# A linear-attention layer gated by a GLU on one core: the down stage's operands loaded ahead from shared half buffers, two sets of down weights' sums moved between passes, folds of q re-spaced

## The chip, the cores and the metric

The kernel runs on one core of a Trainium2 chip. The metric is device time in microseconds (us) of one launch. The core has five engines with a queue each, which take their instructions in order: TensorE (PE, matmuls), VectorE (DVE), ScalarE (ACT), GpSimd (POOL), and SyncE (SP), which issues nearly all the DMAs of this kernel.

## The reference

With x of 2048 rows and 1024 columns, F = 3584, 32 heads of 32:

```python
xn = layernorm(x)
q, k, v = heads(xn @ wqkv)
phi_q = concat(softmax(q @ w_phi), softmax(-(q @ w_phi)))      # phi_k likewise
kv, z = sum_s phi_k[s] v[s], sum_s phi_k[s]
s = concat_heads((phi_q @ kv) / (phi_q @ z + 1e-6)) @ wo
h = sigmoid(xn @ w_gate) * (xn @ w_up)
out = x + s * silu(h @ w_down)
```

All is float32. The kernel makes each float32 product of three matmuls: an operand is split into a rounded part (a cast on ScalarE, L134) and the remainder (a subtraction on VectorE, L135), and L143, L144 and L145 multiply the three pairs that matter.

## The kernel before

**Stages.** Around the big products stands a two by two block scheme with seven products instead of eight (the names B11, B21, B22, T1 to T4), whose operands are sums and differences of blocks. The projections of q, k and v come first, then pass 1 of the gate and up products, then pass 2 (about 1350 to 1640 us), then the down product (to about 2120 us), then the output product and the gate.

**Pass 2** has *nests*: for an f block (128 of the 3584 columns) the T1 operand is itself made by seven products of quarter blocks, `nest(n, f)`. Its weights are loaded by `nest_load` (L518 and L520, from wg_d) and summed on GpSimd four ticks later (L524 to L527); `prep` then splits them with L134 and L135, for the next nest while TensorE is on this one. Inside a nest ScalarE copies banks from one product's place to the next (L1520, L1526, L1538, L1553), and TensorE starts the next product behind such a copy.

**Around it**, GpSimd multiplies the gates (L1415, L1530) and makes the sums of h for the down product (`h_out`, L1385 to L1388); SyncE stores them to h_d (L1378, L1382 and, three ticks later, L1392) and fetches the partial results m_d (L1362).

**Sums of down weights.** The seven down weights of each j in 0..13 are blocks of w_down (B11, B21, B22), or sums of four. `wd_sums(j, b)` loads four blocks (L885), subtracts four times on GpSimd (L875 to L878) four ticks later, and stores four results to wd_d (L882) seven ticks later. j of `WD_B` are made in pass 1 among the groups of sums of w_gu (`glu_group`, `wd_group`), those of `WD_C` in pass 2 every 11 ticks from the 20th, the last four in the down stage.

**Order.** A list `plan` maps ticks to functions; `later(n, f)` puts f n ticks ahead, and `tick()` is called between products. What a tick issues is put behind the last matmul and the latest instructions of VectorE, ScalarE and SyncE at that moment.

**Down stage.** `dsteps` holds 98 steps: 84 with both column halves of h (c = 0, 1) and 14 with one. `down_prep` prepares the next step whenever buffers for splits are free: it loads a weight (L898, 256 KB, from w_down or wd_d) into one of two halves of slot 42, and h (L904, 512 KB for both c; L908, 256 KB, for one) into one of slots 39, 40 and 41, and emits the splits in the same call. The loads of q for the attention (`q_late`) run in this stage on the same queue. SBUF is a row of `slots`, each with two halves; `raw_free` holds the free halves that pass 2's loads share.

**Folds of q**: `fold_steps(at, k)` makes, for a quarter k of the q weights, the products with the feature map, the transforms and the sums.

Of the kernel before, what the change touches and what calls it, by code (L numbers as in the profile page):

```python
# [49 lines left out]
def hedgehog_glu_kernel(  # L50
# [60 lines left out]
    NW = 8  # L111
    WARM = 57
    EARLY = 12
    BEHIND = 'DVE', 'Activation', 'SP'

    banks = [psum.tile([P, HB], F32, name=f"bank{i}") for i in range(8)]

    def whole(i):
        return slots[i].rearrange("p a n -> p (a n)")

    def halves(*ids):
        return [slots[i][:, a] for i in ids for a in range(2)]
# [6 lines left out]
    def pair(i):  # L129
        return slots[i][:, 0], slots[i][:, 1]  # L130
# [39 lines left out]
    def tick():  # L170

        clock[0] += 1
        with behind():
            glu_group()
            nest_load()
            for f, a in sorted(plan.pop(clock[0], []), key=lambda fa: fa[0] is fetch_operand):
                f(*a)

# [198 lines left out]
    def fold_keep(which, k, i, b):  # L377
        nc.sync.dma_start(wf_d[which, i, :, k], b)

    def fold_steps(at, k):  # L380

        def load():
            for n in range(4):
                fold_load(Q, k, n)

        def transforms():
            for n, o in enumerate(halves(*fblock[Q][k])):
                ps = tps.next()
                folded(Q, k, n, ps)
                nc.scalar.copy(o, ps)  # L390

        def sums():
            a11, a12, a21, a22 = bs = halves(*fblock[Q][k])
            for i, b in ((B11, a11), (B21, a12), (T4, a22)):
                fold_keep(Q, k, i, b)
            w_sums(lambda i, b: None, *bs)

        def keep():
            a11, a12, a21, a22 = halves(*fblock[Q][k])
            for i, b in ((T2, a11), (T3, a21), (T1, a22), (B22, a12)):  # L400
                fold_keep(Q, k, i, b)

        for n, f in ((0, load), (4, transforms), (6, sums), (8, keep)):
            later(at + n, f)


# [19 lines left out]
    summed = (T2, T3, T1, B22)  # L426

    FLY = range(2, NJ - 1)
    WD_B, WD_C = range(4), range(4, 10)
    raw_free, spare, groups, made_sums = deque(), [], deque(), {}  # L430
    for f in FLY:
        groups.extend((f, s) for s in range(2))
        if 0 <= f - 4 < len(WD_B):
# [3 lines left out]
    def glu_load(n):  # L437

        if n == len(ops) or ops[n][0] != "glu" or n in wraw:
            return True  # L440
        _, p, f, i = ops[n]
        if p == 1 and f in FLY:
            return True
        src = wg_d[summed.index(i), f] if i in summed else w_gu[f + NJ * (i == T4), int(i != B11)]
        if p == 0:
            r = gr.next()
            last_load[:] = [nc.sync.dma_start(whole(r), src).ins]
            wraw[n] = halves(r)
            return True
        if (p, f, i) == (1, 0, T2):  # L450
            raw_free.extend(halves(41, 42, 39, 40))
        if len(raw_free) < 2:
            return False
        wraw[n] = [raw_free.popleft() for _ in range(2)]
        for s, o in enumerate(wraw[n]):
            last_load[:] = [nc.sync.dma_start(o, src[:, s * HB:(s + 1) * HB]).ins]
        if (p, f, i) == (1, 1, T4):
            spare.extend(halves(43, 44))
            raw_free.extend(spare)
        return True  # L460

# [394 lines left out]
    dsteps = [(i, j, (0, 1)) for i in order[:-1] for j in range(NJ)]  # L856
    dsteps += [(B22, j, (c,)) for c in (0, 1) for j in range(NJ)]
    dready, hfree, wfree = [], deque(), deque()
    hraw = Ring((39, 40, 41))
    wdraw = Ring(halves(42))  # L860
    yr = Ring(halves(47, 48, 49))
    sig_r = Ring([slots[53][:, 0]])
    last_split, down_load = [], []

    def wd_block(i, j):
        f, col = {B11: (2 * j, 0), B21: (2 * j + 1, 0), B22: (2 * j + 1, 1)}.get(i, (2 * j, 1))
# [21 lines left out]
    def wd_sums(j, b):  # L888
        for n, f in zip((4, 7), wd_parts(j, b)):
            later(n, f)  # L890

    def down_prep():
        n = len(dready)
        if n == len(dsteps) or not wfree or len(hfree) < len(dsteps[n][2]):
            return False
        i, j, cs = dsteps[n]
        r = wdraw.next()
        down_load[:] = [nc.sync.dma_start(r, wd_block(i, j) if i in (B11, B21, B22) else wd_d[i, j]).ins]  # L898
        w = wfree.popleft()
        split(pair(w), r)  # L900
        r = hraw.next()
        hs = {}
        if len(cs) == 2:
            nc.sync.dma_start(whole(r), h_d[i, j].rearrange("p c n -> p (c n)"))  # L904
        for c in cs:
            rc = slots[r][:, c]
            if len(cs) == 1:
                nc.sync.dma_start(rc, h_d[i, j, :, c])  # L908
            hs[c] = hfree.popleft()
            last_split[:] = [split(pair(hs[c]), rc).ins]  # L910
        dready.append((w, hs))
        return True


# [507 lines left out]
    def begin_projection(c):  # L1422

        if c == 0:
            for k in range(4):
                fold_steps((1, 2, 5, 6)[k], k)
            for k in range(4):
                o_steps(14 + 10 * k, k, halves(52, 53))
            return
        for t in range(EARLY):  # L1430
            k_steps(1 + 72 * t // EARLY, 0, t)
        for n in range(5):
            queue2(17 + 8 * n, glu_sums, *sums.popleft(), halves(43, 44))

    def begin_pass(p):

        if p == 0:
            for n in range(CTT):
                later(1 + n + 4 * (n > 3), x_stats, n)
            later(19, x_scales)  # L1440
            for q in range(4):
                later(20 + q, x_rows, q)
            for u in range(4):
                later(24 + 12 * u, x_pair, u)
            for n in range(2 * CTT):
                q_steps(2 + 13 * n // 2, n // 2, n % 2)
            queue2(6, glu_sums, *sums.popleft(), halves(43, 44))
        elif p == 1:
            gates_r.items = halves(45, 46)
            gates_r.n = 0  # L1450
            for n, f, *a in ((165, x_nest_load, 0), (166, x_nest_load, 1), (166, x_nest_load, 2), (171, x_nest_load, 3), (170, x_nest_sums, 0),
                             (175, x_nest_sums, 1), (176, x_nest_split, T2), (177, x_nest_split, T3), (179, x_nest_split, T4)):
                later(n, f, *a)
            at = 1
            for t in range(EARLY, 2 * TT):
                k_steps(int(at), *divmod(t, TT))
                at += 7
                if t % TT == TT - 1:
                    k_end(int(at) + 8, t // TT)
                    at += 16  # L1460
        else:
            for n, j in enumerate(WD_C):
                queue2(20 + 11 * n, wd_sums, j, halves(53, 54))

    NEST = {B11: 4, B21: 6, B22: 2, T1: 0, T2: 16, T3: 18, T4: 36}

# [107 lines left out]
    for n, (kind, c, what, i) in enumerate(ops):  # L1574
# [88 lines left out]
                tick()  # L1663
        if flow["item"] == len(items) and flow["made"] - flow["used"] < NW:
            hfree.extend(ws)
            while wfree and down_prep():
                pass

        if phase == 0:
# [32 lines left out]
    for b in range(2):  # L1702
        block(f"x{b}", 4 * b, 4, F32)
    block("x6", 24, 4, F32)
    block("fb", 44, 3, F32)
    qraw.items = [slots[53][:, 1], slots[44][:, 0]]
    yr.items = halves(47, 48, 49, 27)
    eqr.items, zb = [50, 51, 24, 25], (whole(54), whole(26))
    u1, u2 = halves(0, 1, 2, 3), halves(4, 5, 6, 7)
# [12 lines left out]
    def evacuate(i, p):  # L1722

        b = banks[p]
        t = p // 4 * CTT + p % 4
        if i == B11:
            nc.scalar.copy(u1[p], b)
        elif i == B21:
            y = yr.next()
            nc.vector.tensor_copy(y, b)  # L1730
            nc.scalar.copy(b, u1[p])
            later(1 + (p + 1) // 2, gate_out, y, t, 0)
        elif i in (T2, T3):
            nc.scalar.copy((u1 if i == T2 else u2)[p], b)
        elif i == T4:
            gate_out(yr.next(), t + 4, 0, b)
        elif i == T1:
            nc.vector.tensor_add(u2[p], u2[p], b)
            later(1 + 2 * p, gate_out, u2[p], t + 4, 1)
        else:  # L1740
            nc.vector.tensor_add(u1[p], u1[p], b)
            gate_out(u1[p], t, 1)

    ND = len(dsteps)
    for n, j in enumerate(range(10, NJ)):
        later(1 + 14 * n, wd_sums, j, halves(43, 38))
    for hb in range(2):
        later(1 + hb, nc.sync.dma_start, zb[hb], zb_d[hb])
    for n in range(TT):
# [2 lines left out]
    for n, (i, j, cs) in enumerate(dsteps):  # L1752
        w, hs = dready[n]
        if (i, j) == (T2, 0):
            sig_r.items = [slots[53][:, 0]] + halves(38)
        for c in cs:
            for u in range(4):
                p = 4 * c + u
# [7 lines left out]
        hfree.extend(hs.values())  # L1766
        k, odd = divmod(n - (ND - 2 * NJ) - 9, 3)
        if not odd and 0 <= k < 4:

            with tc.issue_after(down_load[0]):  # L1770
                wo_prep(T3, k)
        if n >= ND - 2 * NJ - 8 and len(WO[B21]) < 4 and hfree:
            WO[B21].append(hfree.popleft())
# [7 lines left out]
            wo_prep(*divmod((n - 40) // 2, 4))  # L1781
        if n == ND - 2 * NJ:
            assert len(WO[B21]) == 4
            block("x1", 4, 4, F32R)
            side.extend([lambda k=k: wo_prep(B21, k) for k in range(4)])
            side.extend([lambda u=u: e_load(u) for u in range(2)])
        if n == ND - NJ:
            assert not plan
            block("x6", 24, 4, F32R)
            block("fb", 44, 3, F32R)  # L1790
            step(1000)
            side.extend([lambda fn=fn, a=a: fn(*a) for fn, *a in attend()])
        if len(dready) == ND:
# [2 lines left out]
                    WO[i].append(free.popleft())  # L1796
                    side.append(lambda i=i, k=len(WO[i]) - 1: wo_prep(i, k))
        if n > ND - 2 * NJ:
            step(1 + (n > ND - NJ and n % 2))
    step(1000)  # L1800
    assert len(WO[T1]) == len(WO[T4]) == 4
    block("fa", 39, 4, F32R)
# [169 lines left out]
```

## Time and profile before

| | |
|---|---|
| runs | 2371.30, 2371.32, 2372.62 us, median 2371.32 |
| profiled execution | 2373.14 us, its span 2371.40 us, granted clock 0.996 |
| busy | PE 2348.0 us (99%), PEld 1958.6, DVE 1649.0 (70%), ACT 1182.1 (50%), POOL 1046.7 (44%) |
| DMA | 633.55 MB, mean 267 GB/s, 76.2% of 16 engines |
| chain that ended last | PE 93%, DMA 2%, POOL 1%, DVE 1%, issue 1%, ACT 1% |

The span is the part of the launch that the profile covers; what lies around it is the difference to the time. "L143 <- ACT L1538" reads: the instruction of line 143 waited for the instruction of line 1538 on ScalarE.

### The profile page before, as it was taken

Reading aid. Unit: us, or ns where it says so; the run is one execution under the profiler, and the core shown is the slowest. Engines: PE = TensorE matmul, PEld = TensorE weight load, DVE = VectorE, ACT = ScalarE, POOL = GpSimd, SP = SyncE. Lnnn points to the kernel's source line nnn. Section 1 sums busy time; section 2 is a strip of 40 time slices with the busy share of each in tenths; the row PEclk is TensorE's granted clock in tenths of the full one; section 3 lists DMA queues with packets and bytes.
Section 4 is the critical chain, followed back from the end, with each engine's and each line's share of the span. In section 5 each row is a group of like instructions: output and inputs, shape, how many; then the busy total and the mean of one; then the engine's idle time right before and its main releaser. Section 6 shows DMA issues by size and latency. Waiting matters only on the chain.

```text
span 2371.4 us, 32110 instructions
## 1 busy us (share of the span) xinstructions
PE 2348.0 (99%) x10900; PEld 1958.6 (83%) x10900; DVE 1649.0 (70%) x2083; ACT 1182.1 (50%) x1848; POOL 1046.7 (44%) x737
## 2 busy tenths in 40 slices
PE   9999999999999999999999999989999999999999
PEld 8888888888888888888888888768888888888887
DVE  7625557755688855567766866545989888867776
ACT  7344544454645655555555555433445444355553
POOL 0314216731121044656421777774656343424556
PEclk9999999999999999999999999999999999999999
DMA  8789989976787776887674978779867667776665
GB/s 295 257 305 358 340 302 349 379 277 212 250 281 258 252 275 234 310 290 266 231 234 156 332 266 266 263 259 385 275 243 264 222 214 242 257 254 242 207 202 181
DMA packets 288309, 633.55 MB, mean 267 GB/s; under 512 B 36752, under 2 KB 37008, under 8 KB 283536
## 3 DMA queue, kind: packets, MB, share of 16 engines
q1 hardware_dynamic: 288144, 631.50, 76.2%
q8 instruction: 85, 1.39, 0.2%
q14 instruction: 80, 0.66, 0.1%
HBM read 378.40 MB, written 252.97 MB: 266 GB/s over the span
## 4 chain that ended last, share of the span: by engine, by line
PE 93%; DMA 2%; POOL 1%; DVE 1%; issue 1%; ACT 1%; SPq 0%; POOLq 0%; DVEq 0%; ACTq 0%
PE bank L143 29%; PE bank L144 29%; PE bank L145 29%; PE bank L727 1%; PE bank L375 1%; PE bank L1050 1%; PE bank L1026 1%; PE bank L1300 1%; DMA fc<-w_down 1%; DMA fc<-e_d 1%; DMA h_d<-x 0%; DMA fb<-wqkT 0%; PE bank L243 0%; POOL x L1415 0%; DMA fc<-qkv_d 0%
## 5 line engine op out<-in xcount | busy, mean ns | idle before, releaser
L143 PE MATMUL bank<-x,w 128*128 128x512 f32 x2304 | 898.9, 390 | 7.1 <-ACT bank L1538 7.0
L144 PE MATMUL bank<-x,w 128*128 128x512 f32 x2304 | 898.9, 390 | 0.0
L145 PE MATMUL bank<-x,w 128*128 128x512 f32 x2304 | 897.0, 390 | 0.0
L135 DVE TENSOR_TENSOR w<-fa,w 128x512 fp32r<-128x512 f32 (+2 forms) x437 | 426.8, 984 | 371.5 <-ACT w L134 363.0
L134 ACT CAST w<-fa 128x512 fp32r<-128x512 f32 (+2 forms) x437 | 296.6, 682 | 445.2 <-PE bank L144 345.6
L143 PEld LDWEIGHTS bank<-x,w 128*128 128x128 f32 x2304 | 433.7, 188 | 97.8 <-ACT bank L1538 7.8
L145 PEld LDWEIGHTS bank<-x,w 128*128 128x128 f32 x2304 | 433.6, 188 | 89.9
L144 PEld LDWEIGHTS bank<-x,w 128*128 128x128 f32 x2304 | 433.8, 188 | 89.2 <-DVE x L135 0.4
L143 PE MATMUL bank<-w,x 128*128 128x512 f32 x708 | 277.4, 392 | 0.0
L145 PE MATMUL bank<-w,x 128*128 128x512 f32 x708 | 276.0, 390 | 0.0
L144 PE MATMUL bank<-w,x 128*128 128x512 f32 x708 | 275.9, 390 | 0.0
L145 PEld LDWEIGHTS bank<-w,x 128*128 128x128 f32 x708 | 133.0, 188 | 27.5 <-DVE x L1226 0.3
L144 PEld LDWEIGHTS bank<-w,x 128*128 128x128 f32 x708 | 133.1, 188 | 26.4
L143 PEld LDWEIGHTS bank<-w,x 128*128 128x128 f32 x708 | 133.1, 188 | 26.2
L1370 ACT COPY fc<-bank 128x512 f32<-128x512 f32 x168 | 97.1, 582 | 96.8 <-PE bank L145 52.9
L135 DVE TENSOR_TENSOR x<-fa,x 128x512 fp32r<-128x512 f32 x112 | 105.0, 938 | 28.1 <-ACT x L134 27.8
L134 ACT CAST x<-fa 128x512 fp32r<-128x512 f32 x112 | 69.1, 617 | 61.6 <-DMA fa<-w_down 36.8
L135 DVE TENSOR_TENSOR w<-fb,w 128x512 fp32r<-128x512 f32 (+1 forms) x45 | 40.3, 894 | 48.6 <-ACT w L134 48.6
L1064 POOL TENSOR_TENSOR fc<-fc 128x512 f32<-128x512 f32 x32 | 48.9, 1528 | 56.3 <-DVE fc L1059 20.7
L135 DVE TENSOR_TENSOR p<-fc,p 128x512 fp32r<-128x512 f32 (+1 forms) x67 | 52.2, 790 | 30.6 <-ACT p L134 29.7
L135 DVE TENSOR_TENSOR x<-fb,x 128x1024 fp32r<-128x1024 f32 x36 | 46.1, 1282 | 28.8 <-ACT x L134 28.7
L306 POOL TENSOR_TENSOR fb<-fb 128x512 f32<-128x512 f32 x6 | 8.4, 1396 | 126.3 <-DMA fb<-w_gu 116.9
(393 smaller groups left out, 3576.6 us busy)
## 6 DMA issues: line engine op xcount, KB each, us to landing
m_d<-fc SPq DMA_DIRECT2D x168, 256.0 KB, 3.6
fa<-h_d SPq DMA_DIRECT2D x84, 512.0 KB, 4.3
fa<-wf_d SPq DMA_DIRECT2D x32, 1024.0 KB, 6.3
x<-m_d SPq DMA_DIRECT2D x124, 256.0 KB, 5.0
h_d<-fc SPq DMA_DIRECT2D x104, 256.0 KB, 3.8
fc<-e_d SPq DMA_DIRECT2D x48, 512.0 KB, 5.1
fc<-qkv_d SPq DMA_DIRECT2D x72, 256.0 KB, 4.9
fa<-w_down SPq DMA_DIRECT2D x67, 256.0 KB, 4.1
```

What stands on the lines that cost most here:

```text
L134: nc.scalar.copy(o[0], src)
L135: i = nc.vector.tensor_sub(o[1], src, o[0].bitcast(F32))
L143: nc.tensor.matmul(o, a[0], b[0], start=first, stop=False, **kw)
L144: nc.tensor.matmul(o, a[0], b[1], start=False, stop=False, **kw)
L145: last_mm[:] = [nc.tensor.matmul(o, a[1], b[0], start=False, stop=last, **kw).ins]
L375: nc.tensor.matmul(ps[:, gs], r[:, gs], bd[:, 4 * f + g], start=True, stop=True)
L727: nc.tensor.matmul(kvb[g // 2][:, g % 2 * 256:g % 2 * 256 + 256], v[:, g].rearrange("p a f -> p (a f)"), ph[:, g].rearrange("p a f -> p (a ...
L1026: nc.tensor.transpose(ps[:, j * P:(j + 1) * P], e[:, k * P:(k + 1) * P], ident)
L1050: nc.tensor.matmul(ps[:, j * 256:(j + 1) * 256], kg[:, k], ph[:, a, k], start=a == 0, stop=a == 1)
L1064: nc.gpsimd.tensor_sub(o, a, b)
L1300: nc.tensor.transpose(banks[3][:, a % 4 * P:(a % 4 + 1) * P], ident, ident)
L1370: nc.scalar.copy(o, banks[b])
```

## The change

It does four things.

1. The loads of a down step are parted from its splits. `down_load` takes two or three halves from `raw_free` and issues the load of the weight and one 256 KB load for each half of h; `tick` calls it once the nests' loads are all out. `down_prep` splits a step at least `LEAD` = 2 ticks after its load and gives the halves back. Two halves (slot 44) are kept back at the end for the attention. The rings `hraw` and `wdraw` go.
2. `WD_B` grows from 4 to 6 sets, made in pass 1; the other four of pass 2 come every 16 ticks instead of every 11.
3. The folds of q: the transforms of k = 2, 3 come one tick later, the output folds at 16 + 9k instead of 14 + 10k.
4. Buffers that the attention and the last wd_sums use change place (slots 45 and 46 for 43 and 44), sigmoids get two buffers earlier, the last gates go out one tick instead of two ticks apart.

```diff
+    LEAD = 2
...
             nest_load()
+            if not nests:
+                glu_load(len(ops) - 1)
+            while down_load():
+                pass
...
-    def fold_steps(at, k):
+    def fold_steps(at, k, lead=4):
...
-        for n, f in ((0, load), (4, transforms), (6, sums), (8, keep)):
+        for n, f in ((0, load), (lead, transforms), (lead + 2, sums), (lead + 4, keep)):
...
-    WD_B, WD_C = range(4), range(4, 10)
+    WD_B, WD_C = range(6), range(6, 10)
...
-    hraw = Ring((39, 40, 41))
-    wdraw = Ring(halves(42))
+    ND = len(dsteps)
...
+    def down_back(o):
+        if len(down_loads) > ND - NJ and len(retired) < 2 and any(o is b for b in last_raw):
+            retired.append(o)
+        else:
+            raw_free.append(o)
+
+    def down_load():
+        n = len(down_loads)
+        if nests or len(ops) - 1 not in wraw or n == len(dsteps) or len(raw_free) < 1 + len(dsteps[n][2]):
+            return False
+        i, j, cs = dsteps[n]
+        r, *hr = [raw_free.popleft() for _ in range(1 + len(cs))]
+        last_down[:] = [nc.sync.dma_start(r, wd_block(i, j) if i in (B11, B21, B22) else wd_d[i, j]).ins]
+        for c, o in zip(cs, hr):
+            nc.sync.dma_start(o, h_d[i, j, :, c])
+        down_loads.append((clock[0], r, hr))
+        return True
+
     def down_prep():
         n = len(dready)
-        if n == len(dsteps) or not wfree or len(hfree) < len(dsteps[n][2]):
+        if n >= len(down_loads) or not wfree or len(hfree) < len(dsteps[n][2]):
             return False
...
+        at, r, hr = down_loads[n]
+        if clock[0] < at + LEAD:
+            return False
         w = wfree.popleft()
         split(pair(w), r)
...
-                fold_steps((1, 2, 5, 6)[k], k)
+                fold_steps((1, 2, 5, 6)[k], k, 4 + k // 2)
...
-                o_steps(14 + 10 * k, k, halves(52, 53))
+                o_steps(16 + 9 * k, k, halves(52, 53))
...
-                queue2(20 + 11 * n, wd_sums, j, halves(53, 54))
+                queue2(20 + 16 * n, wd_sums, j, halves(53, 54))
...
-    qraw.items = [slots[53][:, 1], slots[44][:, 0]]
+    qraw.items = [slots[53][:, 1], slots[45][:, 0]]
+    sig_r.items = [slots[53][:, 0], slots[45][:, 1]]
...
-            later(1 + 2 * p, gate_out, u2[p], t + 4, 1)
+            later(1 + p, gate_out, u2[p], t + 4, 1)
...
-        later(1 + 14 * n, wd_sums, j, halves(43, 38))
+        later(1 + 14 * n, wd_sums, j, halves(46, 38))
```

Lines of the new kernel are 5 to 24 higher: the nests' sums L524 to L527 are L530 to L533 there, wd_sums' subtractions L875 to L878 are L880 to L883, h's sums L1385 to L1388 are L1407 to L1410, the gates' products L1415 and L1530 are L1437 and L1552, SyncE's L1392 is L1414, L885 is L890, L518 is L524.

GpSimd in pass 2, between the sums of h (L1385 to L1388) and the sums of the nest's weights that the profile has at 1549.18 to 1553.06 us, before:

```order
L1388 TENSOR_TENSOR fc_100<-x_4_9513,fc_100 128x512
L875 TENSOR_TENSOR fc_100<-fc_100 128x512
L1415 TENSOR_TENSOR x_3_9514<-x_3_9514 128x512
L876 TENSOR_TENSOR fc_100<-fc_100 128x512
L1530 TENSOR_TENSOR x_4_9513<-x_4_9513,fc_100 128x512
L524 TENSOR_TENSOR fa_97<-fa_97 128x256
L877 TENSOR_TENSOR fc_100<-fc_100 128x512
L1415 TENSOR_TENSOR x_3_9514<-x_3_9514 128x512
L525 TENSOR_TENSOR fa_97<-fa_97 128x256
L526 TENSOR_TENSOR fa_97<-fa_97 128x256
```

And the same place after:

```order
L1410 TENSOR_TENSOR fc_100<-x_4_9537,fc_100 128x512
L530 TENSOR_TENSOR fa_97<-fa_97 128x256
L531 TENSOR_TENSOR fa_97<-fa_97 128x256
L532 TENSOR_TENSOR fa_97<-fa_97 128x256
L1437 TENSOR_TENSOR x_3_9538<-x_3_9538 128x512
L533 TENSOR_TENSOR fa_97<-fa_97 128x256
L1552 TENSOR_TENSOR x_4_9537<-x_4_9537,fc_100 128x512
```

The set of wd_sums is no longer here, and the nest's sums stand directly behind the sums of h.

GpSimd at the nest whose sums the profile has at 1499.59 to 1501.83 us, before:

```order
L1387 TENSOR_TENSOR fc_100<-x_3_9514 128x512
L1388 TENSOR_TENSOR fc_100<-x_3_9514,fc_100 128x512
L524 TENSOR_TENSOR fa_97<-fa_97 128x256
L525 TENSOR_TENSOR fa_97<-fa_97 128x256
L526 TENSOR_TENSOR fa_97<-fa_97 128x256
```

And after:

```order
L1410 TENSOR_TENSOR fc_100<-x_3_9538,fc_100 128x512
L880 TENSOR_TENSOR fc_100<-fc_100 128x512
L881 TENSOR_TENSOR fc_100<-fc_100 128x512
L1437 TENSOR_TENSOR fc_100<-fc_100,x_3_9538 128x512
L882 TENSOR_TENSOR fc_100<-fc_100 128x512
L1552 TENSOR_TENSOR x_3_9538<-x_3_9538,fb_99 128x512
L530 TENSOR_TENSOR fa_97<-fa_97 128x256
L883 TENSOR_TENSOR fc_100<-fc_100 128x512
L1437 TENSOR_TENSOR fc_100<-fc_100,x_3_9538 128x512
L531 TENSOR_TENSOR fa_97<-fa_97 128x256
L532 TENSOR_TENSOR fa_97<-fa_97 128x256
```

A set of wd_sums now stands between the sums of h and this nest's sums.

SyncE at the end of pass 2, around the second to fourth down steps' loads, before (L898 loads w_down for a down step, L904 its h, L882 stores to wd_d):

```order
L1392 DMA h_d<-fc_100 128x512
L885 DMA fc_100<-w_down 128x512 x4
L904 DMA fa_97<-h_d 128x1024 x2
L1382 DMA h_d<-x_3_9514 128x512
L1378 DMA h_d<-fb_99 128x512
L1382 DMA h_d<-x_3_9514 128x512
L1392 DMA h_d<-fc_100 128x512
L898 DMA fa_97<-w_down 128x512
L1392 DMA h_d<-fc_100 128x512
L898 DMA fa_97<-w_down 128x512
```

And after (L912 loads w_down for a down step, L914 one half of its h, L887 stores to wd_d, L1400 and L1404 are L1378 and L1382):

```order
L1414 DMA h_d<-fc_100 128x512 x2
L912 DMA fa_97<-w_down 128x512
L914 DMA fa_97<-h_d 128x512
L887 DMA wd_d<-fc_100 128x512 x2
L914 DMA fa_97<-h_d 128x512
L887 DMA wd_d<-fc_100 128x512 x2
L1404 DMA h_d<-x_3_9538 128x512
L1400 DMA h_d<-fb_99 128x512
L912 DMA fb_0_98<-w_down 128x512
L914 DMA fb_0_98<-h_d 128x512
L914 DMA fb_99<-h_d 128x512
```

The down steps' loads of w_down moved ahead of the stores L1392 that follow the next f blocks' sums, and each load of h became two.

More of the change, by code (lines that the diff above doesn't have):

```diff
@@ L428, in hedgehog_glu_kernel @@
     FLY = range(2, NJ - 1)
-    WD_B, WD_C = range(4), range(4, 10)
-    raw_free, spare, groups, made_sums = deque(), [], deque(), {}
+    WD_B, WD_C = range(6), range(6, 10)
+    last_raw, raw_free, spare, groups, made_sums = [], deque(), [], deque(), {}
     for f in FLY:
@@ L457, in glu_load @@
         if (p, f, i) == (1, 1, T4):
-            spare.extend(halves(43, 44))
+            last_raw.extend(halves(44))
+            spare.extend(halves(43) + last_raw)
             raw_free.extend(spare)
@@ L858, in hedgehog_glu_kernel @@
     dready, hfree, wfree = [], deque(), deque()
-    hraw = Ring((39, 40, 41))
-    wdraw = Ring(halves(42))
+    ND = len(dsteps)
     yr = Ring(halves(47, 48, 49))
     sig_r = Ring([slots[53][:, 0]])
-    last_split, down_load = [], []
+    last_split, last_down = [], []
     def wd_block(i, j):
@@ L890, in wd_sums @@
             later(n, f)
+    down_loads, retired = [], []
+    def down_back(o):
[14 more added lines that the diff above has]
+        return True
     def down_prep():
         n = len(dready)
-        if n == len(dsteps) or not wfree or len(hfree) < len(dsteps[n][2]):
+        if n >= len(down_loads) or not wfree or len(hfree) < len(dsteps[n][2]):
             return False
-        i, j, cs = dsteps[n]
-        r = wdraw.next()
-        down_load[:] = [nc.sync.dma_start(r, wd_block(i, j) if i in (B11, B21, B22) else wd_d[i, j]).ins]
+        at, r, hr = down_loads[n]
+        if clock[0] < at + LEAD:
+            return False
         w = wfree.popleft()
         split(pair(w), r)
-        r = hraw.next()
         hs = {}
[L903 to L908, printed above, removed]
+        for c, o in zip(dsteps[n][2], hr):
             hs[c] = hfree.popleft()
-            last_split[:] = [split(pair(hs[c]), rc).ins]
+            last_split[:] = [split(pair(hs[c]), o).ins]
         dready.append((w, hs))
+        for o in (r, *hr):
+            down_back(o)
         return True
@@ L1665, in hedgehog_glu_kernel @@
             hfree.extend(ws)
-            while wfree and down_prep():
+            while down_prep():
                 pass
@@ L1704, in hedgehog_glu_kernel @@
     block("x6", 24, 4, F32)
-    block("fb", 44, 3, F32)
-    qraw.items = [slots[53][:, 1], slots[44][:, 0]]
+    qraw.items = [slots[53][:, 1], slots[45][:, 0]]
+    sig_r.items = [slots[53][:, 0], slots[45][:, 1]]
     yr.items = halves(47, 48, 49, 27)
@@ L1742, in evacuate @@
             gate_out(u1[p], t, 1)
-    ND = len(dsteps)
     for n, j in enumerate(range(10, NJ)):
-        later(1 + 14 * n, wd_sums, j, halves(43, 38))
+        later(1 + 14 * n, wd_sums, j, halves(46, 38))
     for hb in range(2):
@@ L1754, in hedgehog_glu_kernel @@
         if (i, j) == (T2, 0):
-            sig_r.items = [slots[53][:, 0]] + halves(38)
+            sig_r.items = sig_r.items[:2] + halves(38)
         for c in cs:
@@ L1768, in hedgehog_glu_kernel @@
         if not odd and 0 <= k < 4:
-            with tc.issue_after(down_load[0]):
+            if k == 0:
+                block("x1", 4, 4, F32R)
+            with tc.issue_after(last_down[0]):
                 wo_prep(T3, k)
@@ L1783, in hedgehog_glu_kernel @@
             assert len(WO[B21]) == 4
-            block("x1", 4, 4, F32R)
             side.extend([lambda k=k: wo_prep(B21, k) for k in range(4)])
@@ L1787, in hedgehog_glu_kernel @@
         if n == ND - NJ:
-            assert not plan
+            assert not plan and len(retired) == 2
             block("x6", 24, 4, F32R)
             block("fb", 44, 3, F32R)
+            sig_r.items = [slots[53][:, 0]] + halves(38)
             step(1000)
@@ L1798, in hedgehog_glu_kernel @@
         if n > ND - 2 * NJ:
-            step(1 + (n > ND - NJ and n % 2))
+            step(1 + (n > ND - NJ))
     step(1000)
```

## The prediction

> **What bounds the kernel now.** I read the list of what TensorE waits for first, then the table of busy time by 40 us stretch, then the timelines of TensorE, ScalarE, GpSimd and SyncE at each stall. TensorE is busy for 99% of the span, so the only time to be had without taking matmuls away is what it waits, and what its clock loses behind a wait. The list gives waiter, what it waited for, total us, number of waits, longest:
>
> ```profile
> PE bank L143 <- ACT bank L1538: 7.0, 2, 4.9
> PE bank L143 <- ACT bank L1553: 6.2, 1, 6.2
> PE bank L375 <- DMA fb<-wqkT: 1.7, 1, 1.7
> ...
> PE bank L1026 <- DMA fc<-e_d: 1.3, 2, 1.1
> ```
>
> Three waits, 13.2 us together, stand far above the rest. They lie in 120 us of the second pass of the GLU (gate and up products), where the stretches read (us, busy us of PE with its matmuls, PEld, DVE, ACT, POOL, then the clock):
>
> ```profile
> 1480.00:1520.00 40.00, 40.00 (x178) 33.15 (x177) 23.11 (x32) 20.83 (x38) 31.74 (x26) 1.00 0.74 250
> 1520.00:1560.00 40.00, 33.02 (x136) 26.54 (x135) 17.97 (x25) 15.97 (x29) 30.09 (x27) 0.92 0.83 282
> 1560.00:1600.00 40.00, 35.70 (x149) 28.97 (x147) 17.53 (x23) 15.12 (x28) 30.23 (x23) 0.93 0.69 253
> 1600.00:1640.00 40.00, 38.09 (x162) 31.43 (x163) 19.73 (x27) 14.60 (x26) 23.72 (x18) 0.94 1.00 371
> ```
>
> An undisturbed stretch does 178 matmuls, 0.2247 us each. The three disturbed ones do 136 + 149 + 162 = 447 instead of 534: 87 matmuls too few, **19.6 us**. So the stalls cost 13.2 us of waiting and 6.4 us more. Those are clock. TensorE's timeline (start, duration, engine, line; in brackets the idle time before and what ended it) shows it behind the first:
>
> ```profile
> 1531.81 0.50 PE L143 MATMUL bank<-x,w 128*128 128x512 f32 x1 [2.04 <-ACT bank L1538]
> ...
> 1533.70 0.63 PE L144 MATMUL bank<-x,w 128*128 128x512 f32 x1
> 1534.13 0.63 PE L145 MATMUL bank<-x,w 128*128 128x512 f32 x1
> ...
> 1536.69 0.42 PE L145 MATMUL bank<-x,w 128*128 128x512 f32 x1
> 1559.07 0.80 PE L143 MATMUL bank<-x,w 128*128 128x512 f32 x1 [4.94 <-ACT bank L1538]
> 1601.91 0.79 PE L143 MATMUL bank<-p,w 128*128 128x512 f32 x1 [6.21 <-ACT bank L1553]
> ```
>
> After the stall of 2.04 us the starts of matmuls lie 0.43 us apart from 1533.70 to 1536.69, not 0.22: seven intervals, 1.4 us lost though the stall was short. The Trainium skill (TensorE: Matmul & The Clock Gate, "What's actually happening") has the clock fall to half only after an idle window of about 3.4 us; this trace does not agree, since 2.04 us was enough. By the page the first stall would cost no clock and 18.2 us could be had, not 19.6; I go by the count of matmuls.
>
> Why did ScalarE come late? Its timeline shows one cast ahead of each of the three copies that TensorE waited for:
>
> ```profile
> 1526.96 0.62 ACT L134 CAST w<-fb 128x512 fp32r<-128x512 f32 x1 [4.02 <-POOL fb L526]
> 1553.82 0.62 ACT L134 CAST w<-fa 128x512 fp32r<-128x512 f32 x1 [6.52 <-POOL fa L526]
> 1600.22 0.62 ACT L134 CAST x<-fa 128x512 fp32r<-128x512 f32 x1 [10.39 <-DMA fa<-w_down]
> ```
>
> Engines run in order. The first two casts prepare weights of the next nest and wait for its sums (L526) on GpSimd; the bank copies L1538 of the nest that TensorE is on stand behind them. The third is the down stage's first w_down, whose load is late. Of 4.02 us of ScalarE's wait 2.04 reach TensorE, of 6.52 4.94, so the first 1.6 to 2.0 us of lateness are free. GpSimd's timeline shows why the sums are late:
>
> ```profile
> 1543.73 1.30 POOL L875 TENSOR_TENSOR fc<-fc 128x512 f32<-128x512 f32 x1 [7.40 <-DMA fc<-w_down]
> 1553.06 0.73 POOL L526 TENSOR_TENSOR fa<-fa 128x256 f32<-128x256 f32 x1
> ```
>
> A set of wd_sums (L875 to L878) costs 4 × 1.30 = 5.2 us, and its first instruction can hold GpSimd for a late load as well, here 7.40 us. Those loads, and the down stage's, stand on SyncE behind stores (L1392) that wait for GpSimd:
>
> ```profile
> 1537.23 2.94 SPq L885 DMA_DIRECT2D fc<-w_down  x4
> 1540.44 0.96 SPq L518 DMA_DIRECT2D fa<-wg_d  x2
> 1575.05 0.70 SPq L1392 DMA_DIRECT2D h_d<-fc  x1
> 1597.12 0.32 SPq L1392 DMA_DIRECT2D h_d<-fc  x1
> 1597.54 0.38 SPq L898 DMA_DIRECT2D fa<-w_down  x1
> ```
>
> The loads of a set (L885) go out ahead of the next nest's (L518). The store of 1597.12 waited for GpSimd, and the w_down load that ScalarE needed (L898) went out 0.4 us behind it and landed at 1600.2.
>
> **Two sets of wd_sums to pass 1, the rest 16 ticks apart.** Before, sets start on GpSimd ahead of nearly every nest's sums. In the new order two of the last four stand well before 1480, one is before the sums of the nest that runs around 1500, and one behind all nest sums. The two sets that delayed the casts of 1526.96 and 1553.82 are gone from there: each takes 5.2 us and the second 7.40 us of waiting with it. The first cast was 4.02 us late and gains at least 5.2; the second was 6.52 late and gains 5.2 + 7.40 = 12.6. Both fall below the free 1.6 to 2.0 us, so both stalls end: 7.0 us of waiting. What is late next is the set that now sits before an earlier nest:
>
> ```profile
> 1490.27 1.29 POOL L1388 TENSOR_TENSOR fc<-x,fc 128x512 f32<-128x512 f32 x1
> 1499.59 0.73 POOL L524 TENSOR_TENSOR fa<-fa 128x256 f32<-128x256 f32 x1 [8.03 <-DMA fa<-wg_d]
> ...
> 1501.09 0.74 POOL L526 TENSOR_TENSOR fa<-fa 128x256 f32<-128x256 f32 x1
> 1502.45 0.62 ACT L134 CAST w<-fa 128x512 fp32r<-128x512 f32 x1
> 1496.87 2.25 SPq L885 DMA_DIRECT2D fc<-w_down  x4
> ```
>
> Here GpSimd stood idle 8.03 us before L524, and L526 ended at 1501.83, 0.6 us before the cast. The new set's four loads now stand ahead of this nest's load on SyncE (2.25 to 2.94 us by the rows), and two instructions more between L524 and L526 (L878 and a L1415, 2.6 us); the other three subtractions fit in the idle 8.03 us, if their loads have landed. Against that, the set that ran just before this (5.2 us) now runs a nest earlier. 0.6 − 2.94 − 2.6 + 5.2 = +0.3 us: on time to a hair. The bounds: if nothing of the 5.2 us comes through, the cast is 4.9 us late, between the stalls of 2.04 and 4.94 us; if all goes as summed, nothing. I keep 1.4 us for it, nearer the lower end, since lateness up to 1.6 is free.
>
> In pass 1 the two extra sets have room on GpSimd, whose busy us (the fifth) in late stretches of that pass are:
>
> ```profile
> 1200.00:1240.00 40.00, 40.00 (x185) 33.42 (x184) 23.27 (x31) 23.88 (x35) 2.62 (x2) 1.00 0.63 204
> 1240.00:1280.00 40.00, 40.00 (x186) 33.41 (x185) 23.53 (x30) 21.58 (x33) 6.13 (x4) 1.00 0.35 118
> ```
>
> 2.62 and 6.13 of 40 us, as the pass's sums are done well ahead. Two sets cost 10.4 us of that lead, and their 8 loads and 8 stores 16 × 0.38 = 6 us of SyncE. I price it at nothing (a gain is excluded, since TensorE waits for nothing in that pass); without that cover each set could cost up to 5.2 us of TensorE.
>
> **Down operands from the shared half buffers, loaded four steps ahead.** The third down step's w_down load, which went out at 1597.54, now stands right behind the store of 1575.05: some 22 us earlier. ScalarE's wait of 10.39 us ends, and with it the 6.2 us at L1553 and their clock loss. ScalarE's next link there is the cast of the half of h_d, loaded at the same place.
>
> For the 84 steps with two halves, one 512 KB load of h_d becomes two of 256 KB: 84 more on SyncE. In the down stage there is nowhere to hide a late load, since VectorE is nearly full (39.62 of 40 us in the worst stretch):
>
> ```profile
> 1680.00:1720.00 40.00, 39.83 (x176) 32.63 (x175) 39.62 (x56) 18.14 (x32) 25.69 (x18) 1.00 0.84 285
> ...
> fa<-h_d SPq DMA_DIRECT2D x75, 512.0 KB, 4.0
> ...
> fa<-h_d SPq DMA_DIRECT2D x22, 256.0 KB, 3.3
> ```
>
> One step is 24 matmuls, 24 × 0.2247 = 5.4 us. The rows on SyncE cost 0.38 us an issue: 84 × 0.38 = 32 us more of issuing, in 84 × 5.4 = 454 us, on a queue that issues and waits in turn. A load needs 4.0 us to land (3.3 for half of it), and it now has up to four steps, 21.6 us, where three raw buffers gave at most three. So I price it at nothing. The upper bound: if each split came 0.38 us later and VectorE, full, passed all on, 32 us. The Trainium skill (DMA: Bandwidth & Descriptors, "Rules for kernel authors") speaks against this edit: it asks for transfers of a mebibyte or more and small ones joined. The rows agree that a half is not half as dear: two in turn take 6.6 us, one whole 4.0. By the page's rule the down stage would pay up to 84 × 2.6 = 218 us if nothing hid it; by the rows 6.6 us fit into a lead of 21.6, and I keep the price at nothing.
>
> **Edits at nothing.** The folds of q change place by a tick or two; their first load is the wait of 1.7 us at L375, which stays, since the first two folds keep their place. The other buffers of wd_sums 10 to 13, q and the sigmoids change who shares what, with no instruction added. The waits of e_d (1.3 us) stand behind the gate's stores, whose order does not change.
>
> **The sum.** The profiled execution took 2373.14 us, span 2371.40; 2373.14 − 19.6 + 1.4 = 2354.9. The median of the runs, 2371.32, lies 1.82 below the profiled one, so I forecast 2371.32 − 19.6 + 1.4 = **2353.1 us**.
>
> **Rivals.**
> *Stall moved to an earlier nest (18%).* The third set, or the w_down loads ahead of a nest's load, make the cast near 1502 late as bounded above. It would cost up to 4.94 us and a clock loss of the size seen, 6.4 / 3 = 2.1: 7.0 us, in place of my 1.4. 2371.3 − 19.6 + 7.0 = 2358.7; with the third stall left as well (6.2 + 2.1) 2367.0. For it: 0.3 us of room.
> *Nothing gained (7%).* The nests are limited by the cycle of GpSimd's tile sums, SyncE's stores, load and landing, not by wd_sums: 30 of 40 us busy on GpSimd, the rest waits for loads (8.03 us at 1499.59). Without the sets the stalls come at other nests. 2369 to 2373. Against it: up to 1520 the same nests ran without a stall, with sets among them.
> *Slower: SyncE in the down stage (10%).* With 84 more issues and a load that waits for the buffer of four steps before, loads of q and e_d queue behind it; VectorE, full, gets its work late, and TensorE waits at each step. It decides from 18.2 / 84 = 0.22 us a step on. With one issue of 0.38 us a step: 84 × 0.38 = 32 us, 2371.3 − 19.6 + 32 = 2383.7.
> *The forecast's case (65%)*: 2351.7 to 2356.
>
> **Range and chances.** 2349 to 2364 leaves out the slower rival, most of no gain, and little of the second. A measurement can tell some 0.2% (4.7 us) from no change. Faster by more: the first case and nearly all of the second, and nothing of the others: 0.84. Within: 0.06 (no gain, and part of the second). Slower: 0.10.
>
> **What would show it.** Right: the stretches from 1520 on do 178 matmuls at clock 1.00; ScalarE's casts of nest weights never wait over 2 us for GpSimd; the first cast of w_down waits for no load; in the stage after 1640 the list has no new wait of TensorE. Wrong: a wait of TensorE for L1538's copy near 1500, or for splits in the down stage; waits of TensorE in pass 1 for sums of w_gu; or the stalls gone and the time unchanged, which would say that the clock or VectorE set the end.

## The result and the profile after

The changed kernel takes 2355.64 us (median of 6 runs, 2353.72 to 2359.33) against 2371.31: a ratio of 0.9936, 95% interval 0.9923 to 0.9949, or 15.7 us less. In the later comparison it had 2355.89 us and 0.9928 (0.9916 to 0.9940). The profiled execution took 2359.33 us, span 2357.5, the slowest of the six: 13.9 us of span less than before.

The list of what TensorE waits for, after (waiter, releaser, total us, number, longest):

```profile
PE bank L144 <- ACT bank L1560: 3.3, 1, 3.3
...
PE bank L1048 <- DMA fc<-e_d: 1.4, 1, 1.4
PE bank L733 <- DVE p L727: 1.0, 1, 1.0
PE bank L380 <- DMA fb<-wqkT: 0.7, 1, 0.7
```

L1560 is L1538 of before, the copy of a bank within a nest. Of 13.2 us in three waits, one of 3.3 us is left, and the busy time by stretch shows where:

```profile
1480.00:1520.00 40.00, 36.69 (x156) 29.89 (x155) 20.93 (x28) 17.96 (x33) 27.62 (x23) 0.96 0.73 237
1520.00:1560.00 40.00, 40.00 (x178) 33.14 (x177) 24.08 (x32) 20.39 (x38) 27.68 (x24) 1.00 0.80 268
1560.00:1600.00 40.00, 40.00 (x179) 33.10 (x178) 32.89 (x36) 20.72 (x39) 33.29 (x23) 1.00 0.89 307
1600.00:1640.00 40.00, 40.00 (x178) 33.14 (x177) 16.99 (x23) 12.96 (x22) 20.29 (x16) 1.00 0.98 360
```

The three stretches that did 447 matmuls now do 535. The one that was undisturbed, 1480 to 1520, lost 178 − 156 = 22, or 4.9 us. The account of the spans: 19.6 gained, 4.9 lost, 1.0 lost to the new wait of L733, makes 13.7 of the 13.9 measured. It holds for this execution, the slowest of the six. Another of the same kernel, profiled in the later comparison, took 2355.55 us, near the median, and lost less in this stretch: 178 − 169 = 9 matmuls, 2.0 us, behind a wait of 1.7 us.

```profile
1480.00:1520.00 40.00, 38.31 (x169) 31.39 (x168) 24.04 (x30) 20.36 (x37) 28.42 (x23) 1.00 0.77 255
```

How the new stall comes about stands in four timelines (GpSimd, SyncE, ScalarE, TensorE) of the changed kernel at the nest near 1500, from the first of the two executions:

```profile
1485.76 1.62 POOL L1410 TENSOR_TENSOR fc<-x,fc 128x512 f32<-128x512 f32 x1
1497.20 1.30 POOL L880 TENSOR_TENSOR fc<-fc 128x512 f32<-128x512 f32 x1 [9.82 <-DMA fc<-w_down]
...
1503.58 1.18 POOL L530 TENSOR_TENSOR fa<-fa 128x256 f32<-128x256 f32 x1
...
1507.91 0.74 POOL L532 TENSOR_TENSOR fa<-fa 128x256 f32<-128x256 f32 x1
1489.94 0.49 SPq L1414 DMA_DIRECT2D h_d<-fc  x1
1490.49 2.30 SPq L890 DMA_DIRECT2D fc<-w_down  x4
1492.89 1.92 SPq L524 DMA_DIRECT2D fa<-wg_d  x2
1508.68 0.62 ACT L135 CAST w<-fa 128x512 fp32r<-128x512 f32 x1 [4.87 <-POOL fa L532]
1513.95 0.80 PE L144 MATMUL bank<-x,w 128*128 128x512 f32 x1 [3.31 <-ACT bank L1560]
```

GpSimd is done with the sums of h at 1487.4 and then stands for 9.82 us, since the set's loads went out at 1490.49, behind a store. Only at 1497.20 does the set begin, five instructions of 1.3 us stand before the nest's first sum (1503.58), L532 ends at 1508.6, and the cast waits 4.87 us for it.

### The profile page after: what moved, and what is told of

It reads as the page before. It is cut to its first block, busy times and chain, and to the rows that moved or that the text cites. A ratio compares the mean times of both kernels' runs of the same rounds, so it can differ in the third digit from the quotient of the medians.

```text
span 2357.5 us, 32347 instructions
## 1 busy us (share of the span) xinstructions
PE 2343.1 (99%) x10900; PEld 1954.7 (83%) x10900; DVE 1651.5 (70%) x2083; ACT 1181.0 (50%) x1848; POOL 1056.9 (45%) x737
## 4 chain that ended last, share of the span: by engine, by line
PE 93%; DMA 3%; POOL 1%; DVE 1%; issue 1%; ACT 1%; SPq 1%; POOLq 0%; DVEq 0%
PE bank L144 29%; PE bank L145 29%; PE bank L146 29%; PE bank L733 1%; PE bank L1072 1%; PE bank L1048 1%; PE bank L380 1%; DMA fc<-e_d 0%; DMA fb<-wqkT 0%; DMA x<-x 0%; DMA wf_d<-p 0%; DMA fa<-wf_d 0%; DMA fc<-w_down 0%; DMA h_d<-x 0%; PE bank L248 0%
## 5 line engine op out<-in xcount | busy, mean ns | idle before, releaser
L136 DVE TENSOR_TENSOR w<-fa,w 128x512 fp32r<-128x512 f32 (+1 forms) x383 | 372.2, 978 | 356.1 <-ACT w L135 343.5
L135 ACT CAST w<-fa 128x512 fp32r<-128x512 f32 (+1 forms) x383 | 263.8, 691 | 420.8 <-PE bank L145 312.0
L1392 ACT COPY fc<-bank 128x512 f32<-128x512 f32 x168 | 96.9, 583 | 96.5 <-PE bank L146 49.5
L136 DVE TENSOR_TENSOR w<-fb,w 128x512 fp32r<-128x512 f32 (+1 forms) x99 | 96.3, 979 | 65.1 <-ACT w L135 64.9
L135 ACT CAST w<-fb 128x512 fp32r<-128x512 f32 (+1 forms) x99 | 60.8, 615 | 119.6 <-PE bank L145 96.7
L136 DVE TENSOR_TENSOR x<-fb,x 128x512 fp32r<-128x512 f32 (+1 forms) x86 | 95.6, 1112 | 30.9 <-ACT x L135 29.3
L135 ACT CAST x<-fb 128x512 fp32r<-128x512 f32 (+1 forms) x86 | 68.2, 796 | 6.1 <-DMA fb<-w_down 2.9
```

The source lines that it names most:

```text
L135: nc.scalar.copy(o[0], src)
L136: i = nc.vector.tensor_sub(o[1], src, o[0].bitcast(F32))
L1392: nc.scalar.copy(o, banks[b])
```

## The experiments

Ratios are against the kernel before, each in its own comparison, with 95% intervals. The experiments ran in three groups, in which the kernel before had 2372.96 us (the sets alone, the loads alone, a third set, the spacing), 2375.12 (old loads, more DMAs, nine sets, the folds) and 2372.59 (one set, and the three runs side by side).

**The sets alone.** The kernel before, with

```diff
-    WD_B, WD_C = range(4), range(4, 10)
+    WD_B, WD_C = range(6), range(6, 10)
-                queue2(20 + 11 * n, wd_sums, j, halves(53, 54))
+                queue2(20 + 16 * n, wd_sums, j, halves(53, 54))
```

> The kernel before with the sets of wd_sums alone moved (six in pass 1, four in pass 2, 16 ticks apart); the down stage's loads stay as before. Theory of two causes: the stalls near 1530 and 1559 go (7.0 us of waiting and about 4 of clock), a stall of 3.3 us and 1.6 of clock comes near 1514 as in the new kernel, and the wait of TensorE for L1553 near 1600 stays (6.2 and 2.1), since its load still stands behind a store that waits for GpSimd: 2371.3 - 11.2 + 4.9 = 2365. Rival, one cause: the load near 1600 was late only because GpSimd was held by a set of wd_sums in front of that store; then the third stall goes too and the time is that of the new kernel, 2356.

Measured: 2359.36 us, 0.9939 (0.9925 to 0.9952), not to be told from the whole change. TensorE's list and the two stretches that decide:

```profile
PE bank L143 <- ACT bank L1538: 2.3, 1, 2.3
1480.00:1520.00 40.00, 37.71 (x159) 30.68 (x158) 22.59 (x29) 19.19 (x36) 26.68 (x22) 0.96 0.75 250
1600.00:1640.00 40.00, 40.00 (x178) 33.14 (x177) 19.07 (x21) 12.34 (x21) 20.19 (x14) 1.00 1.04 401
```

The rival is right: the third stall went with the sets, though the load stands behind the same store as before. What is left is a wait of 2.3 us near 1510. SyncE shows that the store is not late any more, 1578.02 instead of 1597.12:

```profile
1578.02 0.32 SPq L1392 DMA_DIRECT2D h_d<-fc  x1
1578.43 0.72 SPq L898 DMA_DIRECT2D fa<-w_down  x1
```

**The loads alone.** The new kernel with the two lines of the first experiment as they were before.

> The new kernel with the sets of wd_sums as before (four in pass 1, six in pass 2, 11 ticks apart); the down operands are loaded ahead. Theory of two causes: only the third stall goes, 2371.3 - 8.3 = 2363, and TensorE still waits near 1530 and 1559 for some 7 us. Rival, one cause: what the early loads give is a part of a stall that GpSimd sets, and the time stays within 2 us of 2371. Rival, cost in the down stage: 84 loads more would show as waits of TensorE after 1640 and take the gain away, 2371 or more.

Measured: 2365.55 us, 0.9969 (0.9957 to 0.9980). The first theory's number, 2363, is nearly met: two waits are left, 1.3 us near 1532 and 6.8 us near 1560, and none near 1600.

```profile
PE bank L144 <- ACT bank L1560: 8.1, 2, 6.8
1520.00:1560.00 40.00, 31.93 (x140) 25.75 (x138) 19.44 (x27) 15.27 (x28) 28.94 (x26) 0.97 0.79 271
1560.00:1600.00 40.00, 39.96 (x168) 32.89 (x169) 25.05 (x32) 20.09 (x37) 29.98 (x23) 0.95 0.79 279
1600.00:1640.00 40.00, 40.00 (x178) 33.14 (x177) 17.30 (x23) 11.63 (x21) 23.41 (x18) 1.00 0.95 342
```

So the third stall goes by either half of the change. The gains do not add: 0.61% and 0.31% alone, 0.64% to 0.72% together.

**One set.** To see which set held the store: the kernel before with `range(5), range(5, 10)` in place of `range(4), range(4, 10)`, which takes only the last set of pass 2 away.

> The kernel before with one set of wd_sums only moved: the last of pass 2, whose first subtraction waited 9.38 us near 1584, goes to pass 1; spacing of 11 ticks and the down stage's loads as before. If the third stall was GpSimd's, held by this set in front of the store that the load stood behind, TensorE's wait for L1553 near 1600 goes and the two near 1530 and 1559 stay: 2371.3 - 8.4 = 2363, 0.9965 of before. If the load order alone made it, the wait stays and the time is before's within 2 us.

Measured: 2365.16 us, 0.9967 (0.9955 to 0.9979). TensorE's list has no wait for L1553, and the first two stalls are there, even longer:

```profile
PE bank L143 <- ACT bank L1538: 8.7, 2, 5.5
PE bank L375 <- DMA fb<-wqkT: 1.7, 1, 1.7
```

The last set, alone, was worth 2372.59 − 2365.16 = 7.4 us. So this set made the third stall: in the kernel before, GpSimd waited 9.38 us near 1584 for its loads and then made its four subtractions, and only behind them the sums that the store of 1597.12 waits for.

**A third set moved.** The new kernel, with no set in front of the nest near 1500:

```diff
-    WD_B, WD_C = range(6), range(6, 10)
+    WD_B, WD_C = range(7), range(7, 10)
-                queue2(20 + 16 * n, wd_sums, j, halves(53, 54))
+                queue2((20, 36, 68)[n], wd_sums, j, halves(53, 54))
```

> The new kernel with one more set, the one in front of the nest near 1500, moved to pass 1 (seven there, three in pass 2). Theory: the stall of 3.3 us near 1514 and its clock loss go, 22 matmuls of 0.2247 us: 2355.6 - 4.9 = 2351. Rival: the lead of pass 1 is used up, the seventh set there makes TensorE wait for sums of w_gu or for the statistics of k, one stall of 3 to 7 us: 2354 to 2358. Rival: the cast near 1509 is late for the nest's load alone, and the stall stays: 2355.6.

Measured: 2352.69 us, 0.9910 (0.9896 to 0.9923).

```profile
1480.00:1520.00 40.00, 40.00 (x178) 33.11 (x177) 23.23 (x32) 20.96 (x38) 26.08 (x23) 1.00 0.73 238
1520.00:1560.00 40.00, 40.00 (x178) 33.14 (x177) 25.12 (x31) 20.36 (x38) 31.56 (x25) 1.00 0.82 275
```

No wait of TensorE is left between 1400 and 1640. The four runs lie within 1.6 us of each other; the new kernel's first six spread over 5.6.

**The spacing.** The new kernel with `20 + 11 * n` for `20 + 16 * n`.

> The new kernel with the four sets of pass 2 every 11 ticks, as before, instead of every 16. Theory: the sets now lie where the kernel before had its first four, up to 1520, and ran without a stall; so none near 1500, and what GpSimd has left late of the fourth is caught up, since no set follows: 2351 to 2353. Rival: it is the distance of the sets, not their number, that lets GpSimd catch up; the cast near 1527 is 4 us late as before, TensorE waits 2 us and loses 1.4 of clock, and perhaps again at the next nest: 2355 to 2362.

Measured: 2358.27 us, 0.9929 (0.9916 to 0.9941), not to be told from the new kernel. A wait of 2.2 us stands near 1533 instead of 1514, as the rival had it: the spacing chooses the nest that stalls. My first theory here (no stall) is wrong.

**The early loads once GpSimd is free.** Seven sets in pass 1 and ticks 20, 36, 68, in the kernel before, with its own loads.

> The kernel before with seven sets of wd_sums in pass 1 and three in pass 2 (ticks 20, 36, 68), the down stage's loads as before: 84 DMAs fewer than the run with three sets left and the new loads. What the early loads are worth once GpSimd is free. Theory now, from the run that moved the sets alone: the third stall was GpSimd's, so the early loads give nothing here and this comes out as the run with three sets, 0.991 of before, 2351 to 2353. Rival: without a set to hold the last nests up, the load behind the stores decides again: TensorE waits up to 6.2 us near 1600, 2357 to 2361. Rival: the 84 DMAs more cost something in the down stage, and this is faster than the run with three sets by over 2 us.

Measured: 2356.09 us (2353.24 to 2357.14), 0.9917 (0.9902 to 0.9931), against 0.9910 with the new loads: the same. On one chip, with both and the new kernel:

> The new kernel as it is, beside the others on one chip: 0.9936 of before, with one stall near 1514 of 2 to 4 us in the profiled execution, and a spread of several us between its executions, since the cast there is late by about as much as is free.

> The run with seven sets in pass 1, three in pass 2 and the new loads, again, beside the new kernel and beside the same sets with the old loads: 0.991 of before, no wait of TensorE between 1400 and 1640, faster than the new kernel by some 4 us, executions within 2 us of each other.

> The same sets with the old loads, on the same chip: if the early loads are worth nothing once GpSimd is free, within 1 us of the run above; if they are worth the waits of TensorE seen near 1650 with the old loads (1.1 us and what the executions vary), 1 to 3 us slower than it.

Measured: new kernel 2355.89 us, 0.9928 (0.9916 to 0.9940); three sets 2354.19 us (2353.69 to 2354.89), 0.9920 (0.9907 to 0.9933); the same sets with the old loads 2353.22 us (2350.98 to 2357.52), 0.9918 (0.9905 to 0.9931). The third set is worth less here than the 4 us expected, 1.7, and the intervals overlap; the profiled execution of the new kernel had a stall of 1.7 us only. The medians show no gain from the early loads. What they can do is seen in the execution of 2357.52 us with the old loads, on ScalarE and TensorE:

```profile
1585.18 0.62 ACT L134 CAST x<-fa 128x512 fp32r<-128x512 f32 x1 [6.61 <-DMA fa<-w_down]
1586.86 0.50 PE L143 MATMUL bank<-p,w 128*128 128x512 f32 x1 [2.94 <-ACT bank L1553]
```

The load is still on the edge there; in the execution profiled before, the same cast waited 2.93 us and TensorE not at all near it. With the new loads that wait of TensorE was seen in no profile. The cast that can still wait is the next weight's (2.86 us in the new kernel's first profile), and it stands behind the bank copy. The runs lie closer together in both pairs (1.6 and 1.2 us against 3.9 and 6.5), but other kernels with the new loads spread over 3 to 4 us, so the spread proves nothing.

Off TensorE's path the early loads do much. These rows give who waited for the loads of down weights (us in total, times), before and after:

```profile
  ACT x L134: 59.0, 32
  ACT x L135: 2.9, 1
```

In the five profiles with the old loads these casts of ScalarE waited 41 to 59 us in all, in those with the new at most 4.7. From 1640 to 2120 TensorE, which is what counts, stood for at most 0.8 us with the old loads, and not at all with the new.

The comparison has a weak side: the runs with the new loads carry the new folds and buffers too. With the folds' old lines (below) the new loads had 2351.82 us, against 2356.09 with the old loads in the same group. The intervals overlap, so that a gain of a few us is neither shown nor excluded.

**More DMAs on SyncE.** Three sets and the new loads, with each down weight loaded as two DMAs of 128 KB:

```diff
-        last_down[:] = [nc.sync.dma_start(r, wd_block(i, j) if i in (B11, B21, B22) else wd_d[i, j]).ins]
+        src = wd_block(i, j) if i in (B11, B21, B22) else wd_d[i, j]
+        nc.sync.dma_start(r[:, :256], src[:, :256])
+        last_down[:] = [nc.sync.dma_start(r[:, 256:], src[:, 256:]).ins]
```

> The run with three sets in pass 2 and the new loads, but each of the 98 loads of a down weight is made as two of 128 KB: 98 issues more on SyncE on top of the 84. If the down stage hides the issues (theory), the time stays within 2 us of the run with three sets, 0.991 of before, and TensorE has no new wait from 1640 to 2120. Rival of the prediction, SyncE binds: a part of 98 x 0.38 = 37 us shows, and waits of TensorE for splits appear there; from 3 us on it would count.

Measured: 2354.04 us, 0.9909 (0.9892 to 0.9925), no difference. The edit added more than was said: `dsteps` has 112 entries, not 98 (84 with both halves of h and 28 with one, 14 for each half), and the trace has 224 loads of 128 KB, so 112 issues were added, 112 × 0.38 = 43 us of issuing. TensorE in the whole down stage, first the new kernel, then this one:

```profile
1640.00:2120.00 480.00, 480.00 (x2136) 397.72 (x2135) 414.81 (x591) 219.00 (x363) 227.67 (x160) 1.00 0.75 257
```

```profile
1640.00:2120.00 480.00, 480.00 (x2138) 397.62 (x2137) 421.66 (x596) 221.46 (x366) 225.60 (x160) 1.00 0.78 259
```

**More sets in pass 1.** The new kernel with `range(9), range(9, 10)`.

> The new kernel with nine sets of wd_sums in pass 1 and one in pass 2. Theory: pass 1 has lead to spare; the time is that of the run with seven there, 0.991 of before, within 2 us, as no stall is left in pass 2 to be removed. Rival: the lead of pass 1's sums runs out, and TensorE waits in it for sums of w_gu: 3 us or more slower than with seven.

Measured: 2353.57 us, 0.9910 (0.9895 to 0.9924): as with seven. Pass 1 takes all of them.

**The folds.** Three sets and the new loads, with the folds' old lines.

> The run with three sets in pass 2, with the folds of q spaced as before. Theory: nothing, 0.991 of before within 2 us; TensorE's waits near 145 stay between 0.3 and 1.7 us in either. Rival: the folds hold waits that were not seen in one execution, 1 to 3 us slower.

Measured: 2351.82 us (2350.36 to 2354.21), 0.9901 (0.9887 to 0.9916), the fastest kernel here, though its interval overlaps the others'. Its profile lacks the wait of 1.0 us of L733 for VectorE's L727 near 1078, which the new kernel's and all its other variants' have (1.0 to 1.3 us) and those with the old loads have not. So the wait goes with the folds' new lines, not with the loads. Why the folds' order, 900 us earlier, would decide that is open.

## Why the prediction was right, and where it was not

**The number.** Forecast 2353.1 in 2349 to 2364; measured 2355.64. The sum had 19.6 us of gain and 1.4 of new loss; the profiled execution had 19.6 and 4.9, with 1.0 for a wait that the prediction did not have. By the medians the gain is 15.7 us, where 18.2 was forecast.

**First and second stall: right.** They end when the sets leave (the sets alone: no wait in 1520 to 1600), and stay when the loads alone change (1.3 and 6.8 us).

The nest's load near 1500 on SyncE's timeline of before, for the next point:

```profile
1492.30 0.93 SPq L518 DMA_DIRECT2D fa<-wg_d  x2
```

**The term of 1.4 us was mis-sized.** The prediction counted the set's first three subtractions as hidden in GpSimd's idle 8.03 us, "if their loads have landed". They had not: issued at 1490.49, they landed at 1497.2, so that the idle time was spent waiting (9.82 us) and the subtractions came behind it. The credit of 5.2 us for the set that moved away was real on GpSimd (sums of h done at 1487.4, not 1491.6), but the nest's own load went out no earlier (1492.89, against 1492.30 before), with the set's four loads ahead of it. The cast was 4.87 us late; the bound written down was 4.9, but that is luck, since the bound was made of the nest's load and two instructions, with the three subtractions hidden. It is the stall of the second rival, at its place, and one of the signs of being wrong that were written down. It cost 2.0 us in the execution near the median and 4.9 in the slowest, with 1.7 and 3.3 us of waiting, not 7.0 as the rival was priced. That 2.0 lies near the 1.4 of the sum is luck as well: the reason given for it, hidden subtractions, held in neither execution.

**The third stall: right that it goes, half of why missed.** I gave it to the loads' place on SyncE, and saw that the store waited for GpSimd, but not that a set made GpSimd late. The set at 1584 held the store (one set: 7.4 us; sets alone: gone), and the early loads are a second remedy that is enough by itself (loads alone: 0.31%). Both halves of the change claim the same 8 us; the sum was right because I counted it once, which is luck as far as the cause goes. The late cast of 1600.22 is the third down step's, not the first's as one sentence of the prediction has it.

**The down stage: priced at nothing, right.** 84 loads more left TensorE at 480.00 of 480 us, and 112 more again changed nothing, so the rival that SyncE binds is refuted for this lead. In the new kernel a down weight's load goes out some 18 us ahead of its cast (the median from 1660 to 2080 us), in the kernel before some 7. The Trainium skill's rules to make transfers of a mebibyte or more and to join small ones (DMA: Bandwidth & Descriptors, "Rules for kernel authors") do not show here: 256 KB in place of 512, and 128 in place of 256, with that lead, cost no time that could be measured.

**Pass 1: right.** Five sets more than before (nine) cost nothing there.

**The edits at nothing: one was not.** The folds' new lines bring the wait of 1.0 us at L733. The changed buffers and the gates were not undone alone.

**The early loads: not needed.** Once the sets are gone no gain from them could be told; a wait of TensorE of 2.9 us, which one profiled execution of two with seven sets and the old loads had, was seen in none with the new.

## What to carry to other kernels

When one engine in order serves both urgent and early work, put the early work in a stage where that engine has time to spare, and look at the whole chain of a moved step: here the late landing of the set's loads decided what its arithmetic cost. An idle stretch of an engine is room for moved work only if the work's inputs can be there when it begins; ask what issues them. Two edits that end the same stall are worth it once; undo each alone before adding them up.

## What was not expected of the hardware

Whether the clock falls behind a stall does not follow from the stall's length. In the profiles, idle TensorE of 2.04 us (before) was followed by matmuls 0.43 us apart, and so was 2.17 us with the spacing of 11; one of 2.94 us was not, as TensorE's timeline of the old loads with seven sets and the stretch around it show (14 matmuls too few, 3.1 us, little more than the wait):

```profile
1586.86 0.50 PE L143 MATMUL bank<-p,w 128*128 128x512 f32 x1 [2.94 <-ACT bank L1553]
1587.20 0.40 PE L144 MATMUL bank<-p,w 128*128 128x512 f32 x1
1587.44 0.40 PE L145 MATMUL bank<-p,w 128*128 128x512 f32 x1
1587.68 0.40 PE L143 MATMUL bank<-p,w 128*128 128x512 f32 x1
1560.00:1600.00 40.00, 37.06 (x164) 30.34 (x163) 25.01 (x31) 17.39 (x32) 31.20 (x23) 1.00 0.90 306
```

Against it, the kernel with the spacing of 11:

```profile
1533.03 0.50 PE L144 MATMUL bank<-x,w 128*128 128x512 f32 x1 [2.17 <-ACT bank L1560]
...
1534.65 0.63 PE L146 MATMUL bank<-x,w 128*128 128x512 f32 x1
1535.08 0.63 PE L144 MATMUL bank<-x,w 128*128 128x512 f32 x1
1535.51 0.63 PE L145 MATMUL bank<-x,w 128*128 128x512 f32 x1
```

The Trainium skill (TensorE: Matmul & The Clock Gate, "What's actually happening") has the clock watch a window that runs freely; that would fit a stall of the same size hitting or missing it, though not its 3.4 us of idleness, since 2.04 us were enough. That the window's phase decides was not tried.
